# An attention and Mish kernel on one core: two score tiles of three PSUM banks with the DVE block inside, one projection bank, and PE work placed by an estimated time line

## The chip, the cores and the metric

The kernel runs on one core of one Trainium2 chip. The metric is device time in microseconds (us); lower is better. One execution is also taken by the hardware profiler, and its profile and trace are what is read below.

Engines: PE is TensorE (matmuls), ACT is ScalarE, DVE is VectorE. PSUM is the memory that PE writes its results to, and that ACT and DVE read them from. Both kernels divide it into eight banks of 512 float32 numbers per partition, and all eight are in use.

Some runs of the kernel before fall into a slower state (more than 1.5% above its fastest run of the series, with a lower granted clock). The one profile of the kernel before is of an execution of 997.54 us, still fast by that rule but 7 us above the median of its runs. Its stretches below are longer than usual by about as much.

## The reference, cut to what matters

```python
# x: 1 x 2048 x 640 in bfloat16; 32 heads of width 20
g = sigmoid((x * gate_w).sum(-1, keepdims=True))

# branch A: softmax attention
q, k, v = split_heads(x @ wqkv)
p = softmax(einsum("bhqd,bhkd->bhqk", q, k) * 20 ** -0.5)
a = merge_heads(einsum("bhqk,bhkd->bhqd", p, v)) @ wo

# branch B: dense, Mish, dense
h = x @ w1 + b1                       # 640 -> 1536
b = (h * tanh(log1p(exp(-abs(h))) + where(h > 0, h, 0))) @ w2

return g * a + (1 - g) * b
```

## The kernel before

The work of the attention is cut into *blocks*: 128 keys x 512 queries of one head. There are 2048 of them. A *group* is one chunk of 512 queries with four heads, 64 blocks; there are 32 groups. Four heads share PE, each in its own 32 rows for the scores and in its own 32 columns for the product with V ("PV"; one *quad* is the PV of four blocks).

Most blocks get their exponential from ACT. 232 blocks get it from DVE instead: a first pass reads the score from PSUM and writes int16, then five passes over a pair of blocks in SBUF work out three terms whose sum approximates the exponential. So such a block costs PE three PV matmuls instead of one. All other PE work (the projections q, k, v, the dense layers, `wo`) is called *units* here and is filled in between.

PSUM: a three-bank and a two-bank score tile (`S0`, `S1`), one bank `acc` for PV, and two banks that serve the units **and** the DVE blocks.

```python
WIDTHS = (3, 2)                      # blocks per ACT tile, in turn
DPAIRS = (14, 30, 46, 62)            # where in a group DVE takes a pair of blocks
...
acc = psum.tile([P, QC], F32, tag="acc")
banks = [psum.tile([P, QC], F32, tag=f"bank{i}", name=f"bank{i}") for i in range(2)]
...
def next_bank():                     # the units take the two banks in turn
    ubank[0] ^= 1
    return banks[ubank[0]][:, :]
...
def emit_D(n):                       # one DVE block: its own score matmul, in a unit's bank
    ...
    d = banks[ubank[0] ^ 1]
    bank_free[ubank[0] ^ 1] = now[0] + 1
    scores(d[:, :], blocks[n])
    nc.vector.tensor_scalar(out=A[:, i, :], in0=d[:, :], scalar1=exp_c, scalar2=0.0,
                            op0=ALU.add, op1=ALU.max)
    if i == 1:
        ...
        dve_q.extend(chain(n, A, N, m, B))        # the five passes over the pair
...
def normalise(c, p, t):              # after the last PV of a group
    nc.vector.tensor_copy(out=a, in_=acc[:, :])
    ...                              # four DMAs spread the denominators over partitions
    def part1():                     # reciprocal, four DMAs back to one row per head
        ...
    def part2():
        nc.vector.stream_shuffle(out=rr, in_=rr, mask=[0] * R)
        nc.vector.tensor_tensor(out=oTs[c, p], in0=a, in1=rr, op=ALU.mult)
    later[t + 4] = part1             # in so many ACT tiles from now
    later[t + 8] = part2
```

The main loop goes once round for each ACT tile. The order in which it records instructions is the order in which each engine runs them, because the program is recorded with a manual schedule for PE, ACT and DVE:

```python
for t, ns in enumerate(tiles):
    w = WIDTHS[t % 2]
    E = epool.tile([P, w, QC], BF16, tag=f"E{t % 2}", bufs=3 - t % 2, name="E")
    nc.scalar.activation(E[:, 0:nw, :], sp.pop(t)[:, 0:nw, :], ACT.Exp, scale=escale)
    ...
    if t + 2 < len(tiles):
        emit_S(t + 2)                # scores, two tiles ahead of ACT
    ...                              # at most one emit_D, two DVE passes
    used += pv_quads(...min(tiles[t + 1][0], n_end), t)    # PV of all that is finished
    ...                              # units, within a budget of PE columns per tile
    credit -= pump(min(credit, max(room, 300.0)), 1)
```

The loop of tile `t` already records the PV of tile `t`, except where it would pass a DVE block that is not ready.

The softmax here doesn't subtract the row's maximum and nothing guards it: scores larger than these inputs give would overflow.

## Time and profile before

| | before |
|---|---|
| median of the first three runs | 990.04 us (983.97 to 991.18) |
| profiled span | 995.7 us |
| exponential instructions | 727 |
| ACT idle just before exponentials | 80.5 us |
| mean granted PE clock | 0.902 |

From the page: the span, the busy time of each engine, and two rows of the picture in 40 equal slices (ACT's busy tenths, and the granted PE clock in tenths of full speed, 9 meaning 90% or more).

```profile
span 995.7 us, 15399 instructions
PE 874.1 (88%) x6181; PEld 270.5 (27%) x6250; DVE 647.8 (65%) x1269; ACT 876.3 (88%) x751; POOL 19.0 (2%) x36
ACT  3899999899898989999988999989999997996881
PEclk7999999998699789999967999996999996995877
```

The groups of instructions of ACT, with shapes kept apart. Columns: line, operation, output and input, count | busy us, mean ns of one | idle us of ACT just before them, and what ended it.

```profile
L755 ACT ACTIVATE E<-Sp 128x1536 bf16<-128x1536 f32 x363 | 534.8, 1473 | 54.8 <-PE Sp L576 48.6 <-PE bank_73 L576 2.4 <-PE bank_74 L576 0.7
L755 ACT ACTIVATE E<-Sp 128x1024 bf16<-128x1024 f32 x363 | 381.0, 1050 | 25.6 <-PE Sp L576 16.7 <-PE bank_73 L576 6.0 <-PE bank_74 L576 1.7
```

ACT and PE are both busy for 88%. One more block in an exponential costs 1473 - 1050 = 423 ns. ACT waits for score matmuls for 65 us (the table of waits: total us, count, longest):

```profile
ACT E L755 <- PE Sp L576: 65.3, 85, 4.4
```

The busy time of the engines in four stretches (columns: window, us, busy us and count for PE, weight loads, DVE, ACT, POOL; granted PE clock; DMA share; GB/s). The last two stretches end where the accumulator of group 4 and of group 30 has been copied out.

```profile
400.00:425.00 25.00, 24.10 (x186) 7.76 (x187) 18.94 (x37) 24.99 (x23) 0.00 (x0) 1.00 0.05 14
900.00:925.00 25.00, 25.00 (x124) 5.37 (x124) 11.09 (x21) 17.22 (x15) 0.00 (x0) 0.54 0.01 2
0.00:173.40 173.40, 154.38 (x1297) 62.80 (x1319) 86.97 (x212) 146.76 (x129) 18.50 (x35) 0.96 0.12 37
173.40:946.10 772.70, 686.53 (x4676) 197.21 (x4723) 529.96 (x995) 705.15 (x602) 0.52 (x1) 0.90 0.03 9
```

Where the clock is full, ACT works without a gap (24.99 of 25.00 us). Where it is about half, PE is full all the time and ACT gets too little (17.22 us). The timeline of PE shows where half speed begins (start us, duration us, then what; in brackets the idle time before it):

```profile
811.97 0.38 PE L649 MATMUL acc<-dB,VA 128*32 128x512 bf16 x2
820.35 0.61 PE L576 MATMUL Sp<-qT,kT 32*128 32x512 bf16 x2 [8.00 <-ACT E L755]
...
893.89 0.37 PE L576 MATMUL bank_74<-qT,kT 32*128 32x512 bf16 x1 [0.88 <-DVE dA L600]
894.96 0.39 PE L576 MATMUL Sp<-qT,kT 32*128 32x512 bf16 x2
896.45 0.61 PE L576 MATMUL Sp<-qT,kT 32*128 32x512 bf16 x3
```

At 820 us PE had idled for 8.00 us behind a Mish stage on ACT, and a score group then takes 0.61 us instead of 0.39. The Trainium skill, "TensorE: Matmul & The Clock Gate", Part 1, gives half rate after an idle window of about 3.4 us, which agrees. At 896 us the same happens although the longest gap of the 4 us before is 0.88 us. The trace's clock records, which change in steps of 3.41 us, show what the two have in common. In the step that ends where the clock falls, PE was busy for 2.30 of 3.42 us (0.67):

```profile
892.30:895.72 3.42, 2.30 (x20) 0.72 (x20) 3.35 (x7) 2.80 (x4) 0.00 (x0) 1.00 0.00 0
```

All 17 falls of the clock in this trace came after a step in which PE was busy for at most 0.67 of the time, and one of these steps alone was idle throughout (813.80 to 817.21). It isn't a full rule: three steps of at most 0.67 were not followed by a fall.

### The profile page before, as it was taken

What the parts mean: (1) busy time and instruction counts of PE and PEld (TensorE: products, weight loads), DVE (VectorE), ACT (ScalarE), POOL (GpSimd) and SP (SyncE); (2) the same over time, 40 slices, a digit from 0 to 9 for tenths busy, and PEclk for the clock granted to TensorE, in tenths of its full rate; (3) what the DMA queues carried; (4) which work ended last, traced back from release to release, by engine and by line L of the source; (5) the groups of instructions that cost most, each with busy time, mean ns of one, the idle gap of its engine ahead of it and who ended that gap; (6) DMA issues with size and microseconds to landing.
All of it is one profiled execution on the core that took longest, in us unless ns stands there. A gap on an engine that the chain in (4) does not pass through costs nothing.

```text
span 995.7 us, 15399 instructions
## 1 busy us (share of the span) xinstructions
PE 874.1 (88%) x6181; PEld 270.5 (27%) x6250; DVE 647.8 (65%) x1269; ACT 876.3 (88%) x751; POOL 19.0 (2%) x36
## 2 busy tenths in 40 slices
PE   5999998888898688999979998997998969889894
PEld 2433332222222122332212322221332212221221
DVE  2455646677676567777846876774777764774665
ACT  3899999899898989999988999989999997996881
POOL 6000000000000000000000000000000000000000
PEclk7999999998699789999967999996999996995877
DMA  7100000004000000000000000000000000000000
GB/s 231 16 2 2 1 2 1 1 2 140 21 2 1 1 1 2 15 8 9 2 1 1 2 15 8 8 1 1 2 1 2 1 1 8 9 15 1 2 1 27
DMA packets 22216, 14.18 MB, mean 14 GB/s; under 512 B 15968, under 2 KB 20192, under 8 KB 22144
## 3 DMA queue, kind: packets, MB, share of 16 engines
q1 hardware_dynamic: 20512, 12.16, 4.0%
q0 software_dynamic: 320, 0.82, 0.4%
q8 instruction: 49, 0.80, 0.3%
q10 hardware_dynamic: 1312, 0.20, 0.1%
q14 instruction: 23, 0.19, 0.1%
HBM read 10.04 MB, written 2.62 MB: 13 GB/s over the span
## 4 chain that ended last, share of the span: by engine, by line
PE 45%; ACT 29%; DVE 14%; issue 7%; DMA 3%; SPq 2%; DVEq 0%; ACTq 0%; another core or an unknown queue 0%
ACT E L755 26%; PE Sp L576 13%; PE acc L649 13%; PE bank_74 L366 3%; PE bank_73 L366 3%; DVE dA L600 3%; PE bank_73 L231 2%; PE bank_74 L231 2%; ACT hst L354 2%; PE bank_74 L332 2%; PE bank_74 L576 1%; PE bank_73 L332 1%; DVE dm L626 1%; DVE rrow L685 1%; DMA rrow<-rec 1%
## 5 line engine op out<-in xcount | busy, mean ns | idle before, releaser
L755 ACT ACTIVATE E<-Sp 128x1536 bf16<-128x1536 f32 x727 | 841.0, 1261 | 80.5 <-PE Sp L576 65.3
L576 PE MATMUL Sp<-qT,kT 32*128 32x512 bf16 x1816 | 310.7, 408 | 61.8 <-ACT E L755 52.3
L649 PE MATMUL acc<-E,VA 128*32 128x512 bf16 x1816 | 214.0, 416 | 6.3 <-DVE accS L666 6.0
L576 PEld LDWEIGHTS <-kT 32*128 32x128 bf16 x2048 | 82.4, 92 | 270.1 <-issue 250.0
L600 DVE TENSOR_SCALAR dA<-bank_73 128x512 int16<-128x512 f32 x116 | 79.7, 687 | 104.6 <-PE bank_73 L576 101.0
L600 DVE TENSOR_SCALAR dA<-bank_74 128x512 int16<-128x512 f32 x116 | 79.1, 682 | 72.2 <-PE bank_74 L576 71.7
L649 PEld LDWEIGHTS <-VA 128*32 128x32 bf16 x2512 | 69.4, 96 | 188.1 <-issue 174.9
L626 DVE TENSOR_TENSOR dm<-dm 128x1024 f16<-128x1024 f16 x116 | 79.9, 689 | 2.6
L628 DVE TENSOR_TENSOR dB<-dA,dm 128x1024 bf16<-128x1024 bf16 x116 | 79.4, 684 | 0.0
L576 PE MATMUL bank_74<-qT,kT 32*128 32x512 bf16 x116 | 46.2, 398 | 13.0 <-DVE hst L340 6.4
L623 DVE TENSOR_SCALAR dm<-dm 128x1024 f16<-128x1024 bf16 x116 | 49.9, 430 | 4.0
L619 DVE TENSOR_SCALAR dm<-dA 128x1024 int16<-128x1024 int16 x116 | 49.6, 427 | 4.0
L649 PE MATMUL acc<-dN,VA 128*32 128x512 bf16 x232 | 50.0, 428 | 0.1
L649 PE MATMUL acc<-dA,VA 128*32 128x512 bf16 x232 | 49.4, 423 | 0.0
L576 PE MATMUL bank_73<-qT,kT 32*128 32x512 bf16 x116 | 47.9, 413 | 1.6 <-DVE kT L240 1.6
L649 PE MATMUL acc<-dB,VA 128*32 128x512 bf16 x232 | 49.2, 421 | 0.0
L627 DVE TENSOR_SCALAR dN<-dA 128x1024 int16<-128x1024 int16 x116 | 48.8, 420 | 0.0
L366 PE MATMUL bank_74<-w_sb,hst 128*128 128x320 bf16 x204 | 47.6, 325 | 1.0 <-DVE dA L600 0.6
L366 PEld LDWEIGHTS <-hst 128*128 128x128 bf16 x384 | 28.4, 99 | 61.0 <-issue 56.5
L366 PE MATMUL bank_73<-w_sb,hst 128*128 128x320 bf16 x180 | 41.0, 324 | 1.9 <-DVE dA L600 1.7
L332 PE MATMUL bank_74<-xT,w_sb 128*128 128x512 bf16 x115 | 38.6, 391 | 4.1 <-DVE dA L600 3.7
L666 DVE COPY accS<-acc 128x512 f32<-128x512 f32 x31 | 21.4, 690 | 24.6 <-PE acc L649 24.6
(102 smaller groups left out, 610.4 us busy)
## 6 DMA issues: line engine op xcount, KB each, us to landing
w_sb<-in_B_w_dram SPq DMA_DIRECT2D x2, 1920.0 KB, 11.1
x_sb<-in_A_x_dram SPq DMA_DIRECT2D x4, 640.0 KB, 7.7
out_dram<-ot SPq DMA_DIRECT2D x16, 160.0 KB, 1.8
den<-accS SPq DMA_DIRECT2D x124, 2.0 KB, 1.7
rrow<-rec SPq DMA_DIRECT2D x124, 2.0 KB, 1.7
W_sb<-in_A_wqkv_dram SPq DMA_DIRECT2D x1, 1600.0 KB, 15.1
W_sb<-in_A_wqkv_dram SPq DMA_DIRECT2D x1, 800.0 KB, 8.2
wo_sb<-in_A_wo_dram POOLq DMA_DIRECT2D x4, 200.0 KB, 6.6
```

Source lines behind the costliest of these rows:

```text
L231: nc.tensor.matmul(cell["t"][:, :], lhsT=lhs(kt), rhs=xT[:, kt, c * QC : (c + 1) * QC], start=(kt == 0), stop=(kt == KT - 1),)
L332: nc.tensor.matmul(cell["t"][:, :], lhsT=lw["w1"][:, kt, ft * P : (ft + 1) * P], rhs=xT[:, kt, c * QC : (c + 1) * QC], start=(kt == 0), st ...
L366: nc.tensor.matmul(cell["t"][:, :], lhsT=lhs(k, jj), rhs=rhs(k)[:, cols], start=(k == k0), stop=(k == k1 - 1),)
L576: nc.tensor.matmul(dst, lhsT=kT[R * r : R * (r + 1), p, j * P : (j + 1) * P], rhs=qTs[c, p][R * r : R * (r + 1), :], start=True, stop=True ...
L600: nc.vector.tensor_scalar(out=A[:, i, :], in0=d[:, :], scalar1=exp_c, scalar2=0.0, op0=ALU.add, op1=ALU.max)
L619: lambda: ts(out=m, in0=A, scalar1=0x7F, scalar2=0x3F80, op0=ALU.bitwise_and, op1=ALU.bitwise_or,),
L623: lambda: ts(out=t, in0=mf, scalar1=exp_k, scalar2=exp_k * EXP_M, op0=ALU.mult, op1=ALU.add),
L626: lambda: tt(out=t, in0=t, in1=t, op=ALU.mult),
L627: lambda: ts(out=N, in0=A, scalar1=0x7F80, scalar2=None, op0=ALU.bitwise_and),
L628: lambda: (tt(out=B, in0=Ab, in1=t, op=ALU.mult), done_()),
L649: nc.tensor.matmul(acc[R * r : R * (r + 1), :], lhsT=VA[:, j, p, (DH + 1) * r : (DH + 1) * r + R], rhs=es[r][k], start=(j == 0 and k == 0) ...
L755: nc.scalar.activation(E[:, 0:nw, :], sp.pop(t)[:, 0:nw, :], ACT.Exp, scale=escale)
```

## The change

The intent: make every score tile three banks wide, so that ACT needs fewer and longer instructions, and compute the DVE block's score together with its tile, in the tile's third bank (ACT then reads two banks of that tile, DVE the third). That takes 3 + 3 + 1 (`acc`) banks, so one bank is left for the units. The reciprocal of the denominators is spread by a DMA through device memory instead of a DVE shuffle, and used about 18 us after the end of the group by the estimated time line (before: eight exponentials after it). Above all, PE's filling work is no longer placed by budgets per tile. While recording, the kernel keeps an estimated time line of PE, ACT and DVE (`V`, `s_done`, `e_time` and so on) and places PV and units up to the moment when the next scores are due.

The core of the diff; cuts are marked. (A second counter of buffers, `opool` from 12 to 10, the costs in the queue of units and some due dates changed as well.)

```diff
-    WIDTHS = (3, 2)
-    LEAD = 20
-    DPAIRS = (14, 30, 46, 62)
+    BPT = 3
+    DPOS = (1, 2, 6, 7, 11, 12)
+    SLACK = 0.75
...
-    banks = [psum.tile([P, QC], F32, tag=f"bank{i}", name=f"bank{i}") for i in range(2)]
+    bank = psum.tile([P, QC], F32, tag="bank")
...
-    epool = ctx.enter_context(tc.tile_pool(name="epool", bufs=3))
+    epool = ctx.enter_context(tc.tile_pool(name="epool", bufs=5))
...
     def ahead(n):
-        return tile_at[max(0, n - LEAD)] - 4
+        return tile_at[n] - 5
...
     def emit_S(t):
-        w = WIDTHS[t % 2]
-        sp[t] = psum.tile([P, w, QC], F32, tag=f"S{t % 2}", name="Sp")
+        ns = tiles[t]
+        sp[t] = psum.tile([P, BPT, QC], F32, tag=f"S{t % 2}", name="Sp")
         ...
+        if on_dve(t):
+            dve_score(ns[-1], sp[t][:, BPT - 1, :], t)     # DVE's first pass
...
         def part1():
             ...
-            for r in range(4):
-                nc.sync.dma_start(
-                    rr[R * r : R * r + 1, :].rearrange("o (i n) -> o i n", n=ND),
-                    rec[R * r : R * (r + 1), :],
-                )
+            nc.sync.dma_start(scr.rearrange("r (i n) -> (r i) n", n=ND), rec)
+            nc.sync.dma_start(rr[:, :], bass.AP(v.tensor, v.offset, [[QC, 4], [0, R], [1, QC]]))
 
         def part2():
-            nc.vector.stream_shuffle(out=rr, in_=rr, mask=[0] * R)
...
-        later[t + 4] = part1
-        later[t + 8] = part2
+        later.append((V["dve"] + 6.0, 0.25, part1))
+        later.append((V["dve"] + 18.0, 0.69, part2))
...
     for t, ns in enumerate(tiles):
-        E = epool.tile([P, w, QC], BF16, tag=f"E{t % 2}", bufs=3 - t % 2, name="E")
+        na = len(ns) - on_dve(t)
+        E = epool.tile([P, BPT, QC], BF16, tag="E", name="E")
         ...
         if t + 2 < len(tiles):
             emit_S(t + 2)
...
+        while True:
+            q, u = next_quad(), next_step() if credit > 0 else None
+            behind = 3 * t - 4 * quad[0] >= 10
+            if q and (behind or q[0] + pe_cost(q[1], "V") <= limit) and (
+                not u or q[0] <= V["pe"] + 0.15 or q[0] <= u[0]
+            ):
+                pv_quad()
+            elif u and u[0] + pe_cost(u[1], "P") <= limit:
+                credit -= one_step()
+            elif q and q[0] + pe_cost(q[1], "V") <= limit:
+                pv_quad()
+            else:
+                break
+        while 3 * (t + 1) - 4 * quad[0] > 12 and 4 * quad[0] + 4 <= 3 * (t + 1):
+            while dve_q and next_quad() is None:
+                dve_step()
+            pv_quad()
```

## The prediction

> **What bounds the kernel now.** ScalarE (ACT) is meant to be the bound. The page has it busy for 876 of 995.7 us. 841 us of that is the exponentials (727 instructions, 1816 blocks); the rest is mainly the four Mish stages with their table loads. PE is as busy (874 us), DVE is at 648 us. The table of groups gives 1473 ns for a three-bank exponential and 1050 ns for a two-bank one, so 423 ns per block; in a run without waits twelve tiles take 13.66 us, 2.26 us per 3+2 pair after removing the last one's tail. From that I estimate 363 pairs at 813 us; with 22 us Mish, 10 us table loads, about 22 us of filling at the start and 20 us of tail (ACT does nothing after 974 us) the floor of this structure is about 890 us. So about 105 us are lost. By the table of waits, ACT waits 76 us for score matmuls (85 waits for the score tiles, 16 for the DVE blocks' banks), and isolated instructions lose their overlap.
>
> Where: in 25 us slices at full granted clock ACT is 93 to 100% busy; in slices at 0.54 to 0.82 it is only 69 to 88% busy with PE nearly full. The Trainium skill, "TensorE: Matmul & The Clock Gate", Part 1, says that the PE clock halves after an idle window of about 3.4 us; the trace agrees: PE idles up to 8.0 us behind a Mish stage and score groups then take 0.61 us instead of 0.39. Half-speed time totals about 190 us. PE then cannot feed ACT.
>
> **What the change does.**
> - ACT: 683 tiles instead of 727, about 1811 blocks. Estimate at 1.33 and 0.91 us: 809 us. Practically no gain in work.
> - PE: 44 fewer score groups at about 0.32 us each (start to start in the timeline): -14 us. 232 separate DVE score matmuls vanish; they partly ran beside the score group: -30 us, estimated. Against it, DVE blocks no longer sit two to one PV quad always: about 190 quads with three rounds instead of 116, at 0.21 us a round: +31 us. Net about -15 us: small.
> - DVE: 31 shuffles leave, -22 us; the first pass now holds a score tile's bank, so a late DVE delays scores.
> - One projection bank: 1.07 us of matmuls plus an evacuation of 0.7 us and hand-offs, about 240 units; fits, but two units no longer overlap.
> - Filling order: PE work is placed by an estimated time line, with scores kept ahead of ACT, instead of budgets by tile. This is the main gain. The reciprocal's longer DMA path (about 18 us given, group 25 us) is off the critical path.
>
> **On the critical path.** I expect the full-clock idling to fall by about half (20 to 25 us) and 15 to 20 us from cold stretches, as PE has less to do; the Mish stalls remain, so cold stretches remain. The order model assumes the full clock, so it fails there.
>
> **Prediction: 950 us, range 918 to 985.** Faster by over 2%: 0.75; within 2%: 0.21; slower: 0.04.
>
> **What would show it.** ACT's busy time about 860 us, its wait for score matmuls falling from 76 to about 45 us; exponentials 683; PE busy near 830; ACT 97% or more in full-clock slices; mean clock still 0.88 to 0.93 with dips after the Mish stages; DVE about 625 us.
>
> **What would make it wrong.** Slack on PE may itself lower its clock in more windows (mean clock under 0.88): then no gain. DVE's in-order queue may make scores wait for the first pass (a wait of score matmuls on DVE above 20 us). If the cold stretches largely vanish, about 915 us. A backlog of projections at the end would lengthen the tail beyond 20 us.

## The result, and the profile after

The changed kernel takes 1180.34 us (median of four runs, 1179.7 to 1184.85), beside 990.61 us for the kernel before. A ratio in this text is the mean time of one kernel's fast runs over that of the other's of the same rounds, so it is not quite the ratio of the medians quoted. Here it is 1.193, with a 95% interval of 1.185 to 1.201. The prediction was 950 us: wrong in direction.

| | before | after |
|---|---|---|
| profiled span, us | 995.7 | 1183.0 |
| exponential instructions | 727 | 683 |
| busy time of exponentials, us | 841.0 | 849.6 |
| ACT idle just before exponentials, us | 80.5 | 249.4 |
| PE busy, us | 874.1 | 885.5 |
| mean granted PE clock | 0.902 | 0.875 |
| time until group 4 is finished, us | 173.4 | 230.3 |
| groups 5 to 30, us | 772.7 | 894.1 |
| rest, us | 49.6 | 58.6 |

The same lines of the page after:

```profile
span 1183.0 us, 15591 instructions
PE 885.5 (75%) x6258; PEld 303.6 (26%) x6258; DVE 640.0 (54%) x1221; ACT 884.9 (75%) x707; POOL 18.5 (2%) x35
ACT  2677665677668878887877887878888788778770
PEclk6678987999779898798898889989989998978887
```

No engine has noticeably more work than before; all of them wait more. ACT's groups by form after:

```profile
L782 ACT ACTIVATE E<-Sp 128x1536 bf16<-128x1536 f32 x446 | 621.9, 1452 | 120.3 <-PE acc L676 74.3 <-PE Sp L577 45.4
L782 ACT ACTIVATE E<-Sp 128x1024 bf16<-128x1024 f32 x237 | 237.3, 1022 | 129.1 <-PE acc L676 81.1 <-DVE dA L611 38.8 <-DVE dN L645 3.9
```

The wait for scores (`Sp`) has fallen, from 65.3 to 45.4 us. That sum hides two opposite changes: in groups 0 to 4 it rose from 8.7 to 37.6 us, and in groups 5 to 30 it fell from 54.2 to 7.5. And two waits are there that the kernel before did not have: exponentials that wait for a *PV* matmul (`acc`), and two-bank exponentials that wait for DVE's *first pass* (`dA`). ACT's table of waits after:

```profile
ACT E L782 <- PE acc L676: 155.4, 141, 3.4
ACT E L782 <- PE Sp L577: 45.4, 38, 6.9
ACT E L782 <- DVE dA L611: 38.8, 62, 4.5
```

An exponential reads nothing from `acc`. What it needs of a PV matmul is that it has *finished reading* the buffer `E` that the exponential will overwrite. The timeline of PE, ACT and DVE near 942 us shows how this happens:

```profile
941.56 0.39 PE L577 MATMUL Sp<-qT,kT 32*128 32x512 bf16 x3
...
942.88 1.02 ACT L782 ACTIVATE E<-Sp 128x1024 bf16<-128x1024 f32 x1 [0.47 <-PE acc L676]
943.16 0.39 PE L577 MATMUL Sp<-qT,kT 32*128 32x512 bf16 x3
943.96 0.39 PE L577 MATMUL Sp<-qT,kT 32*128 32x512 bf16 x3 [0.41 <-ACT E L782]
944.28 0.61 PE L676 MATMUL acc<-E,VA 128*32 128x512 bf16 x8
944.79 1.45 ACT L782 ACTIVATE E<-Sp 128x1536 bf16<-128x1536 f32 x1 [0.88 <-PE acc L676]
```

The exponential that starts at 944.79 has had its scores since the group at 943.16. It waits for the PV at 944.28. That PV stands in PE's queue behind the scores at 943.96, which are those of the *next* tile, and these in turn had to wait until the exponential from 942.88 had ended, because they go into the same PSUM tile. So one exponential waits for PV, PV waits for scores, and scores wait for the previous exponential: ACT and PE take turns where they should overlap.

The other wait, early in the program (near 73 us):

```profile
72.06 0.69 DVE L235 CAST kT<-bank 128x512 bf16<-128x512 f32 x1 [3.90 <-PE bank L226]
72.81 0.39 PE L577 MATMUL Sp<-qT,kT 32*128 32x512 bf16 x4 [0.26 <-DVE kT L235]
73.23 1.29 DVE L611 TENSOR_SCALAR dA<-Sp 128x512 int16<-128x512 f32 x2 [0.48 <-PE Sp L577]
74.01 3.28 ACT L782 ACTIVATE E<-Sp 128x1024 bf16<-128x1024 f32 x3 [2.60 <-DVE dA L611]
```

The scores are there at 73.2 us. DVE's first pass takes until about 73.92 (two passes took 1.29 us, one 0.69), and only then does the exponential start, at 74.01. It reads two other banks of the same tile. The first line shows a third effect: the copy of the keys out of the projection bank ends at 72.75, 0.06 us before the scores that need them start, so keys are made just in time.

The stretches of the trace that answer to those before, and one at full clock:

```profile
0.00:230.30 230.30, 176.16 (x1320) 71.29 (x1320) 89.95 (x213) 144.60 (x113) 18.03 (x34) 0.81 0.11 32
230.30:1124.40 894.10, 675.07 (x4712) 218.45 (x4711) 519.98 (x949) 718.63 (x578) 0.52 (x1) 0.90 0.05 16
900.00:930.00 30.00, 21.20 (x174) 8.04 (x174) 17.96 (x33) 23.38 (x20) 0.00 (x0) 1.00 0.03 10
```

At full clock ACT is now busy for only 23.38 of 30.00 us, where it was busy for 24.99 of 25.00 before. So there is a loss where the clock is full, and the clock alone cannot explain it. Of the 187.3 us between the two spans, 56.9 lie in groups 0 to 4, 121.4 in groups 5 to 30, and 9.0 in the rest.

### The theories

The expectations below use these letters.

- **B, buffers of exponentials.** `E` has five buffers in one ring, and PV may lag. The exponential of tile `t` writes over that of tile `t-5`, so all blocks up to number 3t-13 must have been read. The last loop of the diff, in the round of tile `t-1`, guarantees just that (`3t - 4*quads <= 12`) and no more. The last quad that the exponential needs may thus be the *last* thing recorded in that round, behind the scores of tile `t+1`, which need the end of exponential `t-1`. The time line has no term for buffers. Counted in the built program, in the order of PE's instructions: 356 of the 683 exponentials wait for a PV matmul that stands behind their own scores; before, 0 of 727.
- **A, the shared score tile.** The recording layer orders two readers of one PSUM tile on different engines, though they read different banks of it. So 236 exponentials wait for a DVE pass that does not concern them, and DVE runs in order, behind evacuations. (236 is also read in the built program.) The Trainium skill, "PSUM — Partial Sum Buffer", Terms, PSUM bank, forbids two engines on the same bank and quadrant at once. These are different banks, so the hardware rule as the page states it does not ask for this order. No run here shows a collision.
- **C, the single projection bank.** Each unit waits until the one before has been evacuated.
- **D, the denominator path.** The new path saves 31 shuffles on DVE and moves the use of 1/den later.
- Rivals: the cold clock (0.875 against 0.902) as a cause and not a consequence, and the later due dates for keys and queries (`ahead`).

### The profile page after: what moved, and what is told of

Read it like the earlier page. It is cut to its first block, busy times and chain, and to the rows that moved or that the text cites. A ratio compares the mean times of both kernels' runs of the same rounds, so it can differ in the third digit from the quotient of the medians.

```text
span 1183.0 us, 15591 instructions
## 1 busy us (share of the span) xinstructions
PE 885.5 (75%) x6258; PEld 303.6 (26%) x6258; DVE 640.0 (54%) x1221; ACT 884.9 (75%) x707; POOL 18.5 (2%) x35
## 4 chain that ended last, share of the span: by engine, by line
PE 38%; ACT 35%; issue 15%; DVE 11%; DMA 1%; ACTq 0%; DVEq 0%
ACT E L782 33%; PE Sp L577 12%; PE acc L676 10%; PE bank L226 5%; PE bank L361 5%; DVE dA L611 4%; PE bank L327 3%; PE bank L268 2%; DVE kT L235 1%; ACT hst L349 1%; DMA W_100<-in_A_wqkv_dram 1%; DVE qT L237 1%; DVE hst L335 1%; PE bank L207 1%; DVE VA L288 1%
## 5 line engine op out<-in xcount | busy, mean ns | idle before, releaser
L782 ACT ACTIVATE E<-Sp 128x1536 bf16<-128x1536 f32 (+1 forms) x683 | 849.6, 1303 | 249.4 <-PE acc L676 155.4
L611 DVE TENSOR_SCALAR dA<-Sp 128x512 int16<-128x512 f32 x236 | 162.3, 690 | 245.4 <-PE Sp L577 243.9
L361 PE MATMUL bank<-w_sb,hst 128*128 128x320 bf16 x384 | 80.1, 327 | 10.5 <-ACT hst L349 9.2
L676 PE MATMUL acc<-dB,VA 128*32 128x512 bf16 x236 | 78.2, 410 | 9.1 <-DVE dB L646 9.0
L676 PE MATMUL acc<-dN,VA 128*32 128x512 bf16 x236 | 79.5, 416 | 2.3 <-DVE dN L645 2.3
L676 PE MATMUL acc<-dA,VA 128*32 128x512 bf16 x236 | 78.4, 411 | 0.0
L327 PE MATMUL bank<-xT,w_sb 128*128 128x512 bf16 x240 | 73.7, 406 | 1.8 <-DVE hst L335 0.8
L335 DVE TENSOR_SCALAR hst<-bank,b1f 128x512 f32<-128x512 f32 x48 | 36.0, 750 | 45.7 <-PE bank L327 45.7
L226 PE MATMUL bank<-xT,wqp 128*128 128x512 bf16 x155 | 50.9, 430 | 3.8 <-DVE kT L235 3.1
L361 PE MATMUL bank<-wo_sb,oT 128*128 128x320 bf16 x248 | 49.8, 326 | 4.6 <-DVE T_c L387 4.5
```

Of the source, the lines that this page charges most:

```text
L226: nc.tensor.matmul(cell["t"][:, :], lhsT=lhs(kt), rhs=xT[:, kt, c * QC : (c + 1) * QC], start=(kt == 0), stop=(kt == KT - 1),)
L327: nc.tensor.matmul(cell["t"][:, :], lhsT=lw["w1"][:, kt, ft * P : (ft + 1) * P], rhs=xT[:, kt, c * QC : (c + 1) * QC], start=(kt == 0), st ...
L361: nc.tensor.matmul(cell["t"][:, :], lhsT=lhs(k, jj), rhs=rhs(k)[:, cols], start=(k == k0), stop=(k == k1 - 1),)
L611: nc.vector.tensor_scalar(out=A[:, i, :], in0=ps, scalar1=exp_c, scalar2=0.0, op0=ALU.add, op1=ALU.max)
L676: nc.tensor.matmul(acc[R * r : R * (r + 1), :], lhsT=VA[:, j, p, (DH + 1) * r : (DH + 1) * r + R], rhs=es[r][k], start=(j == 0 and k == 0) ...
L782: nc.scalar.activation(E[:, 0:na, :], sp.pop(t)[:, 0:na, :], ACT.Exp, scale=escale)
```

## The experiments

Each was timed in three rounds together with the kernel before. The times given are medians of all four runs; ratios are of fast runs, to the kernel before. The runs fall into four series (e1 to e4, e5 to e8, e9 and e10, e11 and e12), in which the median of the kernel before lies between 989.76 and 994.68 us; times of different series are compared only as closely as that.

### e1: dense layer's h in bfloat16

To give `E` more buffers there must be room in SBUF; even six did not fit in. This run only makes the room, so that the next run has a control.

```diff
-            hsts[c] = late.tile([P, FT, QC], F32, tag="hst", name="hst")
-            actTs[c] = [ ... the float32 tile read as bfloat16 ... ]
+            hsts[c] = late.tile([P, FT, QC], BF16, tag="hst", name="hst")
+            actTs[c] = [hsts[c][:, f0 : f0 + 4, :] for f0 in range(0, FT, 4)]
```

> Control for the next run: the kernel after with the Mish input stored in bf16, which frees 12 KB per partition; five exponential buffers as before, same order on every engine. Every theory: 1180 us, within 10 us.

Measured: 1179.12 us (before: 994.68), ratio 1.192 [1.181, 1.203], correct result. The changed kernel took 1180.34. So the room costs and brings nothing that the runs can tell. Until group 4 is finished it takes 224.0 us, against 230.3 after, although the two programs do the same until then: single profiles scatter by about 6 us here.

### e2: nine buffers

```diff
# on top of e1
-    epool = ctx.enter_context(tc.tile_pool(name="epool", bufs=5))
+    epool = ctx.enter_context(tc.tile_pool(name="epool", bufs=9))
```

The order of instructions on every engine is the same as in e1. Only the buffers that they write to, and so their waits, differ.

> As the control, with nine exponential buffers instead of five; the order of all engines is the same. Theory B (an exponential waits until the PV matmuls of five tiles earlier have read its buffer, and these stand behind its own scores on PE: 356 of 683 exponentials carry such a wait, none in the kernel before): ACT's 155 us of waits on PV matmuls vanish, some come back as waits for scores; 1050 us, 1020 to 1085. Rival (one projection bank and just-in-time keys and queries hold PE, the waits only move): above 1130 us.

Measured: 1049.21 us, ratio 1.059 [1.051, 1.068], correct. So 130 of the 190 us come back with four more buffers. ACT's table of waits:

```profile
ACT E L777 <- DVE dA L606: 64.0, 125, 5.1
ACT E L777 <- PE Sp L572: 61.3, 44, 7.2
```

The wait for PV has vanished from it. The wait for DVE has grown from 38.8 to 64.0 us: behind the longer wait it could not be seen in full. The stretches:

```profile
0.00:230.30 230.30, 175.09 (x1300) 71.90 (x1320) 90.00 (x213) 144.36 (x113) 18.03 (x34) 0.81 0.11 32
230.30:997.30 767.00, 613.81 (x4665) 207.37 (x4711) 519.41 (x948) 709.97 (x578) 0.52 (x1) 0.96 0.06 18
```

Groups 5 to 30 take 767.0 instead of 894.1 us, about what the kernel before takes (772.7; the difference is within the scatter of single profiles). The first five groups have gained nothing (230.3). So B is the cause of the loss in the long middle part and of nothing in the first. And the granted clock in this stretch rose from 0.90 to 0.96 though nothing was done about the clock, so in this stretch the low clock was a consequence of the waits. Worked out from span and mean clock, PE spends 295 us at half speed after the change, 196 before, and 157 here. By the clock records the clock fell 38 times after the change, 37 times in e1 and 16 times here. In groups 0 to 4 the clock stays low (0.81, before 0.96), and how much of the loss there goes through it was not separated.

### e3: DVE's first pass reads SBUF

```diff
# on top of e2, with 8 buffers for room
+    fake = consts.tile([P, QC], F32, tag="fake")          # zeros
         nc.vector.tensor_scalar(
-            out=A[:, i, :], in0=ps, scalar1=exp_c, scalar2=0.0, op0=ALU.add, op1=ALU.max
+            out=A[:, i, :], in0=fake, scalar1=exp_c, scalar2=0.0, op0=ALU.add, op1=ALU.max
```

The DVE blocks are wrong: the pass no longer reads its score, and so no longer shares a tile with ACT.

> Wrong result on purpose: eight buffers, and DVE's first pass reads a constant in SBUF, not the score tile, so that neither the exponential waits for DVE's pass over the same tile (236 of 683 do) nor the next scores. Theory A (sharing the score tile costs at least the 39 us that ACT waited for DVE's pass): 25 to 60 us below the run with nine buffers. Rival (the pass is early enough once the buffers are there): less than 10 us below it.

Measured: 985.84 us, ratio 0.996 [0.984, 1.008]. That is 63 us less than e2, just beyond the range that was expected. (The result passed the comparison although these blocks are not computed, so the comparison is blind to them.) A part of the gain is not A: the pass took 0.42 us from SBUF instead of 0.69 from PSUM, which is 236 x 0.27 = 64 us of DVE's busy time, if not of the critical path. e7 keeps the pass at 0.69 us and meets that doubt. ACT's waits:

```profile
ACT E L779 <- PE Sp L574: 73.2, 63, 6.9
```

Only the wait for scores is left. Groups 5 to 30 take 722.7 us, 50 us *less* than before the change. That doesn't yet show a gain of the wider tiles or of the filling order: the new denominator path with its later use brings the kernel before to 740.4 us in this stretch by itself (e4 below), and the other 18 us stand here with a wrong result and a shorter DVE pass. But it takes 208.5 us to finish group 4 (173.4 before). The timeline there:

```profile
141.21 0.69 DVE L237 CAST kT<-bank 128x512 bf16<-128x512 f32 x1 [0.40 <-PE bank L228]
141.96 0.60 PE L574 MATMUL Sp<-qT,kT 32*128 32x512 bf16 x5 [0.79 <-DVE kT L237]
142.45 1.45 ACT L779 ACTIVATE E<-Sp 128x1536 bf16<-128x1536 f32 x1 [2.97 <-PE Sp L574]
```

ACT stood still for 2.97 us, because the keys of these scores left the projection bank only just before.

### e4: the new denominator path alone

The kernel before, with the DMA through device memory, without the shuffle, and with `part2` at `t + 16` instead of `t + 8`.

```diff
-        rr = rrow
+        rr = npool.tile([P, QC], F32, tag="rr", bufs=1, name="rr")
...
+            nc.sync.dma_start(scr.rearrange("r (i n) -> (r i) n", n=ND), rec)
+            nc.sync.dma_start(rr[:, :], bass.AP(v.tensor, v.offset, [[QC, 4], [0, R], [1, QC]]))
...
-            nc.vector.stream_shuffle(out=rr, in_=rr, mask=[0] * R)
...
-        later[t + 8] = part2
+        later[t + 16] = part2
```

> The kernel before with only the new path of 1/den (through a DRAM scratch, used 16 tiles later, no shuffle). Theory: off the critical path, 990 us within 10 us. Rival (the 256 KB transfers or the later use hold something): 1010 us or more.

Measured: 970.89 us, ratio 0.978 [0.968, 0.988], correct. That is outside both expectations: faster than either. Groups 5 to 30 take 740.4 us. This part of the change is not among the causes of the loss; it is a gain of about 2%.

### e5: the kernel before with one projection bank

```diff
     def next_bank():
-        ubank[0] ^= 1
-        return banks[ubank[0]][:, :]
+        return banks[0][:, :]
...
-            bank_free[ubank[0]] = now[0] + 2
+            bank_free[0] = now[0] + 2
...
-        if now[0] and bank_free[ubank[0] ^ 1] > now[0]:
+        if now[0] and bank_free[0] > now[0]:
...
-        d = banks[ubank[0] ^ 1]
-        bank_free[ubank[0] ^ 1] = now[0] + 1
+        d = banks[1]                 # the DVE blocks have the other bank to themselves
...
-        if lead <= LEAD and gap <= 0 and (bank_free[ubank[0] ^ 1] <= t or lead < LEAD - 6):
+        if lead <= LEAD and gap <= 0:
```

> The kernel before with all projection units in one PSUM bank, the other kept for DVE's scores. Theory C (one bank makes every unit wait for the evacuation of the one before, which in the projection-heavy first five groups cannot be hidden): slower by 10 to 45 us, most of it in groups 0 to 4. Rival (the lost first groups of the kernel after come from its later due dates for keys and queries, not from the bank): within 5 us of the kernel before.

Measured: 1042.2 us (before: 990.74), ratio 1.052 [1.040, 1.065], correct. One bank fewer for the units, as placed here, costs the kernel before 5%, 51 us, more than the 10 to 45 that were expected. Two things besides the bank are in this. The kernel's own rule closes a bank for two tiles after its unit (`bank_free`), so from group 1 on, units that no deadline forces start in every second tile at most where only one bank is left. And the condition for a DVE block is looser. What share the bank has was not separated. The one profile fell in the slow state (1055.47 us), so its sizes are not set against fast ones. As a picture only: group 4 is finished at 245.7 us there.

### e6: earlier due dates

```diff
# on top of e3
     def ahead(n):
-        return tile_at[n] - 5
+        return tile_at[max(0, n - 20)] - 4
```

> The run with eight buffers and DVE reading SBUF (wrong on purpose, 986 us), with the due dates of keys and queries as in the kernel before (20 blocks earlier). Rival of theory C (due dates): 20 us or more faster, in groups 0 to 4. Theory C (the bank limits how fast units can be made, whatever their due date): within 10 us of 986.

Measured: 983.11 us, ratio 0.996 [0.989, 1.004]; e3 had 0.996 as well. Group 4 is finished at 208.1 us (208.5 in e3). So these due dates are not the cause of the slow start.

### e7: the score tile cut in two, with the right result

```diff
# on top of e2
-        sp[t] = psum.tile([P, BPT, QC], F32, tag=f"S{t % 2}", name="Sp")
+        sp[t] = (
+            psum.tile([P, 2, QC], F32, tag=f"S{t % 2}", name="Sp"),
+            psum.tile([P, 1, QC], F32, tag=f"T{t % 2}", name="Sq"),
+        )
...
-            dve_score(ns[-1], sp[t][:, BPT - 1, :], t)
+            dve_score(ns[-1], sp[t][1][:, 0, :], t)
...
-        nc.scalar.activation(
-            E[:, 0:na, :], sp.pop(t)[:, 0:na, :], ACT.Exp, scale=escale
-        )
+        ps = sp.pop(t)
+        nc.scalar.activation(E[:, 0:2, :], ps[0][:, :, :], ACT.Exp, scale=escale)
+        if na == 3:
+            nc.scalar.activation(E[:, 2, :], ps[1][:, 0, :], ACT.Exp, scale=escale)
```

ACT and DVE no longer share a tile. The price: a full tile takes two exponential instructions.

> A right result without the shared score tile: nine buffers, each score tile cut into one of two banks and one of one bank, the exponential of a full tile in two instructions. Theory A: ACT's 64 us of waits for DVE's pass go to 0, against about 45 us for 447 more instructions (estimate: 204 ns fixed, less 0.1 us overlap); 1030 us, 1005 to 1050. Rival (the 63 us gained when DVE read SBUF came from its shorter pass or from scores that no longer wait for DVE): 1065 us or more.

Measured: 1003.28 us, ratio 1.017 [1.009, 1.025], correct. It is 46 us below e2 (42 by the two ratios, since the series differ), in spite of the price, and just under the range that was expected, because the price was lower than I had taken it: where ACT does not wait, the next tile follows a full one after 1.38 us instead of 1.33 us (medians of the two traces), 0.05 x 446 = 23 us, where I had estimated 45. ACT's waits:

```profile
ACT E L782 <- PE Sq L573: 48.3, 50, 6.1
ACT E L782 <- PE Sp L573: 11.9, 7, 3.0
```

No DVE any more. This shows A with right results: the order of two readers by tile, and not only the faster pass of e3, cost time. A rival is that the cut frees the first two banks of a tile earlier; but ACT's wait for scores did not fall with it (61.3 us in e2; 63.0 here, 2.8 of them in a line that is not shown), so the gain does not show there. Group 4 is finished at 199.6 us and groups 5 to 30 take 746.0 us. So cutting the tile has taken up to 31 us off the first part (230.3 in e2) and 21 us off the middle (767.0).

### e8: only the later use

```diff
# the kernel before; shuffle and DMAs as they were
-        later[t + 8] = part2
+        later[t + 16] = part2
```

> The kernel before with only the use of 1/den moved from 8 to 16 tiles after the group's end; the shuffle and its transfers stay. The new path alone gave 971 us. Theory D (DVE's 22 us of shuffles, at a busy place, were what gave 2%): no gain, 985 to 997. Rival (the later use spreads DVE work at the group's end): 970 to 980.

Measured: 970.5 us (before: 990.74), ratio 0.983 [0.976, 0.990], correct. e4 had 970.89. So theory D in the form of "31 shuffles saved" falls: the later use alone gives the gain, with all the shuffles still in place. ACT's waits, and the stretches:

```profile
ACT E L755 <- PE Sp L576: 41.0, 70, 3.5
```

```profile
0.00:173.00 173.00, 156.94 (x1318) 63.62 (x1319) 86.71 (x212) 146.87 (x129) 18.73 (x35) 0.97 0.12 37
173.00:911.90 738.90, 668.06 (x4724) 195.98 (x4723) 528.05 (x995) 702.76 (x603) 0.52 (x1) 0.93 0.03 10
```

ACT waits for scores for 41.0 us instead of 65.3; groups 5 to 30 take 738.9 us instead of 772.7, with a granted clock of 0.93 instead of 0.90.

### e9: two projection banks, first try (wrong result)

The eight banks allow two for the units if the third blocks of all tiles share one bank: 2 + 2 (`S0`, `S1`), 1 (`T`), 1 (`acc`), 2 for units.

```diff
# on top of e7
-    bank = psum.tile([P, QC], F32, tag="bank")
+    banks = [psum.tile([P, QC], F32, tag=f"bank{i}", name=f"bank{i}") for i in range(2)]
...
-            psum.tile([P, 1, QC], F32, tag=f"T{t % 2}", name="Sq"),
+    st[t] = psum.tile([P, 1, QC], F32, tag="T", name="Sq")     # in emit_T(t), one bank for all
```

> The run with split tiles (1003 us, right result), its two one-bank tiles made one that is shared by all tiles, and the bank that this frees given to the projections as their second. Theory C (the single bank costs the 35 us that the kernels of this family still lose in groups 0 to 4 against the kernel before): 970 us, 955 to 985, groups 0 to 4 done by 180 us instead of 200. Rival (sharing the third bank makes the scores wait, or the loss at the start lies in the order of filling): 1000 us or more.

Measured: 999.61 us, ratio 1.012, and a wrong result (relative error 0.034). The mistake: with two banks a unit of the second dense layer was recorded before the Mish that it reads. The time was also above the expected range, by 15 us. Group 4 was finished at 172.3 us, as expected by 180. e11 repeats it properly.

### e10: use at 12

```diff
-        later[t + 8] = part2
+        later[t + 12] = part2
```

> The kernel before with 1/den used 12 tiles after the group's end; at 8 it is 990 us, at 16 it was 970 us. If it is the distance (the two DVE operations at the group's end crowd the work there): between, 972 to 985. If it is which DVE block the two operations fall beside: as at 8 or worse, 986 or more, or as at 16, 972 or less.

Measured: 984.58 us (before: 989.76), ratio 0.997 [0.992, 1.002], correct. By the median it is at the edge of what the distance was to give; by the ratio it cannot be told from the kernel before.

### e11: two projection banks, right result

```diff
# on top of e9
     def ready(key):
+        if key[0] == "w2" and key[1] not in mished:
+            return False
```

> The run with two projection banks, mended: a unit of the second linear layer no longer stands ahead of the Mish stage that it reads (that had made the result wrong). Its time was 1000 us, with groups 0 to 4 done at 172 us (200 with one bank) and the later groups 27 us slower than with one bank. Theory C for the early groups alone, with the shared third bank giving the gain back later: 995 to 1005 us, groups 0 to 4 done at 170 to 176 us again, PE waiting over 100 us for the one-bank exponential. Rival (the wrong order had made these numbers): another split, or under 985 us.

Measured: 999.18 us (before: 990.1), ratio 1.010 [1.005, 1.015], correct. Group 4 is finished at 173.1 us: the slow start is gone (as in e9). This is C: 199.6 us with one bank, 173.1 with two. ACT's waits for scores in this part say the same: 37.1 us in e7, 9.4 here, and 8.7 in the kernel before. The two longest of each, e7 first:

```profile
ACT E L782 <- PE Sq L573: 24.1, 16, 6.1
ACT E L782 <- PE Sp L573: 11.0, 5, 3.0
ACT E L803 <- PE Sp L584: 6.0, 7, 2.1
ACT E L803 <- PE Sq L584: 2.2, 5, 0.7
```

The order of the score matmuls changed as well (`emit_T`), so the 26 us are not the bank's alone by proof. All three numbers that were expected came out. But groups 5 to 30 now take 772.1 us instead of 746.0, and the time as a whole hardly differs from e7. ACT's waits for scores rose there from 25.8 to 33.9 us. PE's table of waits shows what stands behind it:

```profile
PE Sq L584 <- ACT E L803: 136.8, 237, 7.3
```

The shared third bank is free for the next tile's third block only after ACT's one-bank exponential. What one projection bank costs in the beginning, one score bank fewer seems to cost later. All eight banks are in use in either version.

### e12: use at 20

```diff
-        later[t + 8] = part2
+        later[t + 20] = part2
```

> The kernel before with 1/den used 20 tiles after the group's end (8: 990, 12: 985, 16: 970 us). If the use only has to be late: 970 or less. If it has to fall between DVE blocks: 978 or more.

Measured: 983.57 us, ratio 0.995 [0.988, 1.003], correct. With e8 and e10 the series for a use after 8, 12, 16 and 20 tiles is 990, 985, 970.5 and 984 us. If 1/den simply came too late at 8, then 12 and 20 would also be fast. They are not, so the distance alone does not explain the gain. That what counts is next to which other instructions the two of DVE fall is an inference; with which ones was not found, and the cause of this gain stays open.

### What was not tried

Recording DVE's first pass behind the exponential of the same tile, as another way round A, did not get through the build (a deadlock in the order), and was not run.

### The account

Time in us until group 4 is finished, and for groups 5 to 30, from one profile each (the one of the kernel before some 7 us above its median):

| kernel | until group 4 | groups 5 to 30 | what differs |
|---|---|---|---|
| before | 173.4 | 772.7 | |
| after | 230.3 | 894.1 | |
| e1 | 224.0 | 894.1 | room only |
| e2 | 230.3 | 767.0 | B gone |
| e3 | 208.5 | 722.7 | B and A gone (wrong) |
| e7 | 199.6 | 746.0 | B and A gone, two instructions per full tile |
| e11 | 173.1 | 772.1 | B, A and C gone, one score bank fewer |
| e4 | 173.7 | 740.4 | before, with the new denominator path, used at 16 |
| e8 | 173.0 | 738.9 | before, with 1/den used at 16 |

The first part of the loss, 56.9 us, is thus A with 22 to 31 us (e3, e7) and C with about 26 us (e11 against e7), which adds up to 48 to 57 (with a scatter of some 6 us in this part, see e1, and with what goes through the clock inside both). The middle part, 121.4 us, is B alone (127.1 us with nine buffers). A costs 21 to 44 us there as well, but gains hide it: the denominator path with its later use is worth 32 us in this stretch by the profiles (e4; 20 us of the whole by the runs), and what the wider tiles and the filling order add to that was not separated.

## Why the prediction was wrong

**"Filling order: PE work is placed by an estimated time line, with scores kept ahead of ACT ... This is the main gain."** This is the step that failed. The estimate has times for the score tiles, for the bank and for `acc`, but none for the buffers of `E`. I looked at whether it keeps PV out of the way of the scores; I did not ask *what a late PV holds back*. PV that may lag by 12 blocks holds four tiles of `E`, and there are five buffers. In place of a wait of 20 to 25 us less, the runs showed a new wait: 155.4 us of exponentials waiting for PV after, none in e2, and 130 us of time that came back with the buffers. That the filling order is a gain in itself, let alone the main one, is not shown: with A and B gone and a right result, groups 5 to 30 take 746.0 us (e7), and the kernel before with the denominator path alone takes 740.4 (e4). The 722.7 us of e3 have a wrong result and a shorter DVE pass.

**"A late DVE delays scores."** The direction was mistaken. I looked for score matmuls that wait for DVE, and put a limit of 20 us on it. What waits is the *exponential of the same tile*, because the two readers of one tile are ordered. That is 38.8 us in the profile after, 64.0 us once B is out of the way. It could have been read before: both readers take slices of one tile `sp[t]`, and the kernel before takes care to give the DVE block a bank of its own.

**"One projection bank ... about 240 units; fits, but two units no longer overlap."** I summed the load and found room. But in groups 0 to 4 the keys and values are needed as soon as they are made, and there it is the latency of one unit and its evacuation that counts, not the load. ACT's wait for scores rose from 8.7 to 37.6 us there. The kernel before loses 5.2% with one bank (e5, with what is said there), and e11 gives about 26 us back in this part.

**"The reciprocal's longer DMA path ... is off the critical path."** The longer path, net of the shuffles that it saves, costs nothing, as I said (e4 and e8 are equal). But the later use is not neutral: e8 is 1.7% faster than the kernel before. Since 12 and 20 tiles do not give this, slack alone does not explain it.

**Right, by luck, and missed.** Right was ACT's work: 683 exponentials as stated, busy 849.6 us against 841.0 before ("practically no gain in work"); with the rest ACT was busy for 884.9 us, where 860 was predicted. The wait for score matmuls fell to 45.4 us, where "about 45" was predicted, but by luck: it rose by 28.9 us in groups 0 to 4, fell by 46.7 in groups 5 to 30, and part of it was hidden behind the wait for PV (61.3 us in e2, without that wait). ACT was to be busy for 97% or more at full clock, and was for 78% (23.38 of 30.00 us). PE's busy time was predicted near 830 us and was 885.5, the lower clock included; with B gone and a clock of 0.96, PE's busy time in groups 5 to 30 is 613.8 us instead of 675.1. DVE's 640.0 us was near the 625 predicted. The mean clock of 0.875 was at the edge of what I had called a sign of no gain (under 0.88), but it followed the waits: it rose with the waits that were taken away (page mean 0.925 in e2, 0.947 in e3) and with no edit to the clock's causes.

**Best version.** Neither the changed kernel nor any repair of it beats the kernel before by a margin that the runs bear out. The kernel before with one number changed (e8, 970.5 us) does so by 1.7%, 1.0 to 2.4% by the interval; with the new denominator path as well (e4, 970.89 us) it is no different.

## What to carry to other kernels

Before you let one engine's work slide, count the buffers that it holds back: what is guaranteed at the end of each round should leave at least one tile of slack over what the next producer needs, and it should stand *ahead* of anything that waits for the producer before. An order made with a time line is only as good as its list of resources, and buffers and shared tiles belong on it. And a load that fits in the sum can still be late: where each result is needed at once, count the latency of one unit through its single bank.

## What the Trainium skill lacked or had wrong

- "TensorE: Matmul & The Clock Gate", Part 1: it gives half rate after an idle window of about 3.4 us and full rate after a busy one. The first agrees at 820.35 us of the kernel before (8.00 us idle, then 0.61 us per score group). But only one of the 17 falls in this trace came after a step of 3.41 us that was idle throughout; the others came after steps in which PE was busy for up to 0.67, as at 895.72 us, where the longest gap was 0.88 us. The page does name short idles between groups of matmuls as a cause of oscillation, but gives no number by which this could be foreseen. By its rule for the way back the clock should be full again after one busy window; it stays at 0.54 from 900 to 925 us while PE is busy for 25.00 of 25.00 us, and 21 of the steps at half speed in this trace were busy for 0.99 or more and yet followed by another one. (Busy is by the matmul records, whose ends are modelled.)
- "ScalarE: Activation LUTs", What ACT_TABLE_LOAD costs: with immediate operands it gives 186 ns + 0.833 ns per element, which is 1039 and 1466 ns for 1024 and 1536 elements. The trace has 1050 and 1473 ns before, 1022 and 1452 after: it agrees. For instructions back to back it gives an overlap of about 93 ns, so one more instruction would cost about 93 ns (an estimate from the page). Measured by e7 against e2 it is about 50 ns per tile (1.38 against 1.33 us).
- "PSUM — Partial Sum Buffer", Terms: the collision rule is by bank and quadrant. It lacks a word that a recording layer may order two readers by *tile*, which is coarser. It cost up to 64.0 us of ACT's waits here (e2), and cutting the tile into two took it away (e7).
- "Perfetto Trace Analysis", Identifying Performance Opportunities, Optimization Strategy: it names the same gap repeating on one engine as a possible sign of too few buffers. It lacks the sign by which it was found here: an exponential that is released by a matmul whose result it does not read (155.4 us after, `E <- acc`; none with nine buffers, e2).
